# An order table in place of a list planner, and doubled values loaded by 128-partition transfers, in an attention and feed-forward kernel

## The chip, the core and the metric

The kernel runs on one core of one Trainium2 chip. TensorE (PE) multiplies matrices, VectorE (DVE), ScalarE (ACT) and GpSimd (POOL) do elementwise work, and SyncE (SP) issues most of the transfers; ScalarE issues some too. Each of these engines works through its own queue in the order in which the program was written, and waits on semaphores where a step needs another engine's result. Sixteen DMA engines move the data. The time is the device time of one execution in microseconds (us); lower is better.

## The reference

Eight sequences of 576 tokens with eight heads of width 64 go through masked attention, and the 4608 x 512 result through a feed-forward layer:

```python
scores = scale * np.matmul(q, k.transpose(0, 1, 3, 2))
mask_local = (rel >= 0) & (rel < stride)                      # heads 0-3, stride 32
mask_strided = (rel >= 0) & (pos[None, :] % stride == pos[:, None] % stride)   # heads 4-7
attn = softmax(np.where(masks, scores, -1e9)); x = np.matmul(attn, v)
h = x @ w_in                          # 512 -> 1024
solu = h * softmax(h)
ln = (solu - mean(solu)) / sqrt(var(solu) + 1e-6) * g_ln
return ln @ w_out                     # 1024 -> 512
```

`q`, `k`, `v` and `g_ln` are 4-byte floats; `w_in` and `w_out` are 8-byte floats.

## The kernel before, in words

**Attention.** For every sequence `b` there are five units of work (`UNITS`): two strided ones (the positions are permuted so that a head's residue classes are contiguous blocks of 18) and three local ones (three blocks of 64 queries with 96 keys each). A unit (`unit`, L492 to L586) computes scores on TensorE (`qk`, L509), takes the maximum and subtracts it on VectorE (L523, L524), exponentiates on ScalarE (L525), sums (L526), normalizes on GpSimd (L534), splits the probabilities into a high and a low half-precision part (L540, L542 or L544), has SyncE transpose them by DMA (`pt<-p`, L546), multiplies with the values (`pv`, L552 to L569) and splits the result into `xhi` and `xlo` (L584, L585).

**Values.** They too are needed as high and low parts, scaled by a power of two that is found from their sum of squares (`v_scale`, `v_split`). The strided values of a sequence are 768 KB as loaded, the local ones 640 KB (`vrl`). For sequence 0 the strided values are loaded twice over, into both halves of the partitions of `vtwo` (`load_v`, L425), so that the product with the high part and with the low part can be stacked; these two loads, `t0` and `t1`, are the first steps on ScalarE's queue. For sequence 0 the sum of squares comes from TensorE (`gram`, L367: each 128-column piece times itself, L379), over `vtwo` first and `vrl` second; the scale is known after that, and both value splits wait for it. For later sequences the second copy is made by transfers inside the chip (`vd<-vtwo`, `ve<-vl`, L486).

**Feed-forward.** 36 tiles of 128 tokens (`ff`, L589). The first matrix product (`g1`, L623, two halves of twelve matmuls) uses high and low parts of both operands; then come maximum, exponential, product, centring, a norm whose power is on GpSimd, a DMA transpose of the centred tile (`ct<-c`, L665), the second product (`g2`, L668) and the scaled store (L677). Tile 0 needs units 0, 1 and 2 of sequence 0 and all of `w_in`.

**Weights.** Each 8-byte float is decoded to 4 bytes in three steps (`decode`, L686: two on ScalarE, one on VectorE), `w_in` in four blocks of 128 rows, `w_out` in four of 256; then squared, scaled and split (`prep_w`, `prep_o`, `split_o`).

**What sets the order.** `add` records each of 1390 steps with its engine, an assumed duration, a key and what it reads and writes. `Plan.order` (L160) plays the steps through on the host: each engine takes, of the steps that are ready by the assumed times, the one with the smallest key; a small model of two shared transfer queues (`Queues`) gives the landing times. Keys stand in the lists `UK`, `PK`, `TK`, `GK`, `VK`, `LK`, `LF`, `LW`, `SK`. `emit` then writes the program in that order. Waits between engines are put in from the data that each step touches, whatever the order.

Of the kernel before, what the change touches and what calls it, by code (L numbers as in the profile page):

```python
# [43 lines left out]
LOAD = (8, 0.35, 1.2, 1.4)  # L44
# [3 lines left out]
LATE0 = 0.5  # L48
POOL_LO = 2
KX = -0.4  # L50
AFTER_O = [1, 1, 2, 2]
ACTQ = {"t0", "t1"}
# [3 lines left out]
UK = [  # L56
    -1.43, -0.93, -24.14, 0.24, -23.81, 0.24, -2.58, 11.29, 49.63, 17.93, 11.81, 0.92, 6.04, 10, 9.99, 12.38, 9.89, 12.65, 11.22, 13.19, 9.73, 11.19,
    20.74, 11.38, 12.09, 0.52, 12.71, 32.96, 19.98, 34.88, 33.33, 33.25, 32.84, 12.73, 26.99, 29.5, 22.87, 22.19, 31.76, 34.07,
]
PK = [  # L60
    -0.48, 11.9, -0.29, 0.88, 15.34, -1.75, -0.14, 1.46, 1.14, 0.3, -0.78, -1.14, -1.42, -6.92, 11.93, 13, 10.91, 13.83, 11.36, 4.85, 11.64, 12.7,
    12.02, -0.87, 11.97, 13.04, 13.11, 12.49, 12.49, 11.54, 11.3, 31.63, 35.51, 32.29, 37.06, 18.48, 32.43, -1, 23.48, 33.16,
]
TK = [
    0.05, 12.2, 31.9, -2.4, -0.23, -0.05, 0.24, -1.38, -0.25, 12.28, -1.81, 11.47, 10.98, -9.03, 10.67, 0.03, 12.6, 12.77, 13.16, 19.1, 30.58, 11.13,
    12.61, 32.31, 32.29, 12.99, 31.83, 31.97, 32.36, 31.96, 30.78, -3.83, 25.23, 32.01, 32.18, 67.85,
]
GK = [
    0.81, 12.13, 53.42, 0.52, 0.39, 0.81, -30.98, 1.04, -1.13, 20.08, 12.59, 32.04, 12.25, 8.26, 10.1, 9.89, 31.45, 12.29, 36.36, 31.27, 12, 36.6,
    10.78, 13.83, 33.09, 31.32, 36.94, 33.12, 33.09, 17.87, 32.04, 33.08, 52.82, 32.68, 33.96, 34.25,  # L70
]
VK = [
    0, 10.56, 12.41, 6.42, 11.99, 28.75, 3.12, 36.73,
]
LK = [
    0, 34.17, -12.99, 12.55, 12.62, 11.03, 25.29, 42.8,
]
LF = [
    -33.99, -14.63, -28.94, -18.35, 0.01, -0.82, 11.84, 1.74, 0.11,
]  # L80
LW = [
    7.65, 31.97, -0.38, -4.92, -24.77, 12.63, -0.92, -0.04,
]
SK = [
# [9 lines left out]
class Queues:  # L94


    def __init__(self):
        self.free = [3.0, 3.0]
        self.busy = [[], []]

    def move(self, q, t, work):
        mine, other = self.busy[q], self.busy[1 - q]
        start = now = max(t, self.free[q])
        shared = 0.0
        for a, b in [x for x in other if x[1] > start]:
            if work <= 0:
                break
            if b <= now:
                continue
            if a > now:  # L110
                alone = min(work, a - now)
                now, work = now + alone, work - alone
                if work <= 0:
                    break
            both = min(b - now, 2 * work)
            now, work, shared = now + both, work - both / 2, shared + both
        self.free[q] = now = now + max(work, 0.0)
        mine.append([start, now])
        if shared > 0:
            self.free[1 - q] += shared / 2  # L120
            other[-1][1] += shared / 2
        return start, now


class Plan:

    HOP = 0.4  # L130
    LATE = 3.0
    DEEP = 100
    SKIP = {"act": 0.1, "dve": 0.08, "pe": 0.07, "pool": -0.1}
# [5 lines left out]
    def add(self, eng, dur, fn, key, r=(), w=(), lock=None, dma=None, after=()):  # L139

        n = len(self.steps)
        deps = set(after)
        for x in r:
            if x in self.writer:
                deps.add(self.writer[x])
        for x in w:
            if x in self.writer:
                deps.add(self.writer[x])
# [6 lines left out]
        lock = eng == "pool" if lock is None else lock  # L155
        self.spaces.append({x[0] for x in (*r, *w) if isinstance(x, tuple) and x[0] in BANKED} if eng in ("pe", "act", "dve") else set())
        self.steps.append((eng, dur, fn, key, deps, lock, dma))
        return n

    def order(self):  # L160
        steps = self.steps
        left = [len(s[4]) for s in steps]
        users = [[] for _ in steps]
        for n, s in enumerate(steps):
            for d in s[4]:
                users[d].append(n)
        ready_at = [0.0] * len(steps)
        free = dict.fromkeys(("pe", "act", "dve", "pool", "sp"), 0.85)
        locked = dict.fromkeys(("dve", "pool"), 0.0)
        queues, moved, pieces = Queues(), 0, []  # L170
        waiting = {e: [] for e in free}
        for n, s in enumerate(steps):
            if not left[n]:
                waiting[s[0]].append(n)
        out = []
        while len(out) < len(steps):
            best = None
            for e, ns in waiting.items():
                if not ns:
                    continue  # L180
                now = max(free[e], min(ready_at[n] for n in ns))
                n = min((n for n in ns if ready_at[n] <= now), key=lambda n: (steps[n][3], n))
                if best is None or now < best[0]:
                    best = now, e, n
            now, e, n = best
            waiting[e].remove(n)
            out.append(n)
            dur = steps[n][1]
            if e == "act" and steps[n][6]:
                _, issue, begins, lands = steps[n][6]  # L190
                end = queues.move(1, now + begins, dur)[1] + lands + (LATE0 if now < 20 else self.LATE)
                free[e] = now + issue + 0.06
            elif e == "sp":
                pushes, issue, begins, lands = steps[n][6]
                start, landed = queues.move(0, now + begins, dur)
                pieces.append((start, landed, moved, moved + pushes))
                moved += pushes
                free[e] = now + issue + 0.06
                for a, b, c, d in reversed(pieces):
                    if c < moved - self.DEEP <= d:  # L200
                        free[e] = max(free[e], a + (b - a) * (moved - self.DEEP - c) / (d - c))
                        break
                end = landed + lands + (LATE0 if steps[n][6] == LOAD and now < 20 else self.LATE)
            else:
                if steps[n][5]:
                    now = max(now, locked["pool" if e == "dve" else "dve"])
                    locked[e] = now + dur
                end = now + dur
                free[e] = end - (0.16 if dur > 2.4 else self.SKIP[e])
            for m in users[n]:  # L210
                left[m] -= 1
                ready_at[m] = max(ready_at[m], end + (0.0 if steps[m][0] == e and not (e == "act" and steps[n][6]) else self.HOP))
                if not left[m]:
                    waiting[steps[m][0]].append(m)
        self.span = max(free.values())
        return out


def emit(nc, tc, plan):
# [4 lines left out]
    for n in plan.order():  # L224
        eng = plan.steps[n][0]
        k = len(nc.cur_bb.bb.instructions)
        plan.steps[n][2]()
# [3 lines left out]
        for x in sorted(plan.spaces[n]):  # L231
            true = [d for d in sorted(plan.steps[n][4]) if x in plan.spaces[d] and plan.steps[d][0] != eng]
# [12 lines left out]
def attn_solu_kernel(ctx: ExitStack, tc: tile.TileContext, qloc, qstr, kloc, kstr, vloc, vstr, w_in, w_out, g, masks, out):  # L245
# [75 lines left out]
    sk = iter(SK).__next__  # L321

# [44 lines left out]
    def gram(dst, pieces, key, w, room, scrap):  # L367
# [4 lines left out]
        for i, (x, r) in enumerate(pieces):  # L372
# [11 lines left out]
            key(), r=[A, "unit"], w=[J, w])  # L384

    def pow2_scale(dst, parts, one, key, r, w, room, top=14, mul=1.0):

        tot, T = room  # L390
# [460 lines left out]
```

## Time and profile before

| | us |
|---|---|
| median of 3 runs (513.05 to 514.99) | 514.79 |
| the profiled execution | 512.79 |
| its span, first to last instruction | 511.1 |
| TensorE busy | 473.5 |
| VectorE busy | 358.5 |
| ScalarE busy | 295.5 |
| GpSimd busy | 157.4 |

The profile is of one execution. In a table by stage each row gives the stretch, its length, busy time of PE, PEld (weight loads, which overlap matmuls), DVE, ACT and POOL with the number of instructions, the granted TensorE clock (1.00 is full speed), the mean busy share of the 16 DMA engines and what they moved in GB/s. A row in order of time is start, duration, engine, line, operation, output <- input, and in brackets how long the engine sat idle before it and what ended that. A row of waits is who waited for whom: total us, times, longest. A row of DMA issues ends with KB each and the median us from issue to landing. L379 is line 379.

### The profile page before, as it was taken

The numbers are of one execution on the slowest core, as the hardware profiler recorded it, in microseconds if no ns is written. First come the engines' busy times: TensorE is split into PE (matmuls) and PEld (weight loads), VectorE is DVE, ScalarE is ACT, GpSimd is POOL, SyncE is SP. The second block draws the span as 40 slices with busy tenths as digits, with TensorE's granted clock in tenths as the row PEclk, the third lists the DMA queues.
The fourth block names the chain that finished last, engine by engine and source line by source line (L and its number), as shares of the span: only waits on it lengthen the run. The fifth ranks groups of instructions, "written<-read, shape, count | busy, mean of one in ns | idle before, by whom it ended". The sixth has DMA issues, their size and how long they took to land.

```text
span 511.1 us, 11878 instructions
## 1 busy us (share of the span) xinstructions
PE 473.5 (93%) x4858; PEld 247.2 (48%) x4858; DVE 358.5 (70%) x679; ACT 295.5 (58%) x414; POOL 157.4 (31%) x258
## 2 busy tenths in 40 slices
PE   0538978999999999999999999999999999999997
PEld 0435544445545555454544455555544555544443
DVE  0597989768767779667994789677975789754330
ACT  1578967684546737654765666564666447554331
POOL 3164363314313214313341235212531315311210
PEclk9855989999999999999999999999999999999999
DMA  8999999739993799979885499979985697673342
GB/s 218 402 310 271 355 211 202 152 77 242 273 199 84 157 211 280 222 212 195 236 161 109 118 227 239 245 202 223 231 158 104 164 167 158 108 122 63 65 104 78
DMA packets 168294, 96.51 MB, mean 189 GB/s; under 512 B 138032, under 2 KB 154800, under 8 KB 167728
## 3 DMA queue, kind: packets, MB, share of 16 engines
q1 hardware_dynamic: 162768, 84.74, 77.9%
q10 hardware_dynamic: 5472, 11.01, 6.9%
q8 instruction: 38, 0.62, 0.5%
q14 instruction: 16, 0.13, 0.1%
HBM read 40.03 MB, written 9.44 MB: 97 GB/s over the span
## 4 chain that ended last, share of the span: by engine, by line
PE 80%; DMA 7%; DVE 5%; ACT 4%; issue 2%; POOL 1%; ACTq 0%; POOLq 0%; DVEq 0%
PE h_ps L626 11%; PE o_ps L670 11%; PE h_ps L628 11%; PE h_ps L627 11%; PE o_ps L671 10%; PE o_ps L672 10%; PE s_ps L517 5%; PE x_ps L568 5%; DMA pt<-p 3%; DMA vtwo<-vstr 3%; PE s_ps L512 2%; DMA ct<-c 2%; POOL t L534 1%; ACT w L712 1%; PE s_ps L672 1%
## 5 line engine op out<-in xcount | busy, mean ns | idle before, releaser
L626 PE MATMUL h_ps<-w,xhi 128*128 128x512 f16 x280 | 107.1, 382 | 0.6 <-DVE eu L647 0.6
L627 PE MATMUL h_ps<-w,xhi 128*128 128x512 f16 x280 | 106.7, 381 | 0.0
L628 PE MATMUL h_ps<-w,xlo 128*128 128x512 f16 x280 | 106.6, 381 | 0.0
L670 PE MATMUL o_ps<-obuf,ct 128*128 128x512 f16 x272 | 103.4, 380 | 1.0 <-DMA ct<-c 1.0
L672 PE MATMUL o_ps<-obuf,ct 128*128 128x512 f16 x272 | 103.1, 379 | 0.0
L671 PE MATMUL o_ps<-obuf,ct 128*128 128x512 f16 x272 | 103.1, 379 | 0.0
L534 POOL TENSOR_TENSOR t<-t,m 128x576 f32<-128x576 f32 (+2 forms) x40 | 56.2, 1404 | 139.4 <-DVE m L531 111.4
L633 DVE TENSOR_REDUCE st<-h_ps 128x1 f32<-128x1024 f32 x35 | 42.8, 1222 | 42.5 <-PE h_ps L628 42.5
L652 DVE SCALAR_TENSOR_TENSOR c<-eu,st,c 128x1024 f16<-128x1024 f32 x36 | 48.8, 1354 | 25.3 <-ACT c L651 24.1
L644 ACT ACTIVATE eu<-h_ps,st,vsc 128x1024 f32<-128x1024 f32 x31 | 37.3, 1204 | 43.3 <-DVE st L634 43.3
L651 ACT ACTIVATE c<-eu,st 128x1024 f16<-128x1024 f32 x36 | 41.2, 1146 | 28.0 <-DVE st L650 26.0
L647 DVE SCALAR_TENSOR_TENSOR eu<-h_ps,st,eu 128x1024 f32<-128x1024 f32 x35 | 44.8, 1280 | 8.8 <-ACT eu L644 8.4
L660 POOL TENSOR_SCALAR st<-st 128x1 f32<-128x1 f32 x36 | 18.7, 520 | 103.2 <-ACT junk L654 102.0
L540 ACT CAST p<-t 128x576 f16<-128x576 f32 (+2 forms) x40 | 26.9, 674 | 33.2 <-POOL t L534 32.6
L628 PEld LDWEIGHTS <-xlo 128*128 128x128 f16 x288 | 28.3, 98 | 34.5 <-issue 0.8
L672 PEld LDWEIGHTS <-ct 128*128 128x128 f16 x288 | 28.2, 98 | 34.0
L626 PEld LDWEIGHTS <-xhi 128*128 128x128 f16 x288 | 28.2, 98 | 33.7 <-DVE eu L647 0.7
L670 PEld LDWEIGHTS <-ct 128*128 128x128 f16 x288 | 28.1, 98 | 33.1 <-DMA ct<-c 1.1
L627 PEld LDWEIGHTS <-xhi 128*128 128x128 f16 x288 | 28.3, 98 | 31.3 <-issue 0.6
L517 PE MATMUL s_ps<-k,q 64*54 64x54 f32 (+1 forms) x1280 | 41.4, 271 | 2.2 <-DMA q<-qloc 2.2
L671 PEld LDWEIGHTS <-ct 128*128 128x128 f16 x288 | 28.2, 98 | 30.2
L654 ACT ACTIVATE junk<-eu,st 128x1024 bf16<-128x1024 f32 x36 | 40.9, 1137 | 0.8 <-ACT ob L678 0.8
(148 smaller groups left out, 707.6 us busy)
## 6 DMA issues: line engine op xcount, KB each, us to landing
out<-ob ACTq DMA_DIRECT2D x36, 256.0 KB, 3.9
vtwo<-vstr SPq DMA_DIRECT2D x7, 768.0 KB, 6.6
vd<-vtwo SPq DMA_DIRECT2D x14, 384.0 KB, 8.8
vrl<-vloc SPq DMA_DIRECT2D x8, 640.0 KB, 5.6
q<-qstr SPq DMA_DIRECT2D x8, 594.0 KB, 5.4
k<-kstr SPq DMA_DIRECT2D x8, 594.0 KB, 6.8
k<-kloc SPq DMA_DIRECT2D x8, 576.0 KB, 6.0
q<-qloc SPq DMA_DIRECT2D x8, 576.0 KB, 4.2
```

The lines of the kernel that those rows point to most:

```text
L517: nc.tensor.matmul(s_ps[row : row + nq, pair, i * nk : (i + 1) * nk], q_raw[half][hs, q0 : q0 + (nq - 1) * nqb + 1 : nqb], k_raw[half][hs, ...
L534: add("pool", nx * nk / 510 + 0.02, lambda: nc.gpsimd.tensor_tensor(tv, tv, sm.unsqueeze(2).broadcast_to([P, nx, nk]), op=ALU.mult), key + ...
L626: nc.tensor.matmul(hv[:, i], xhi[:, cc, tok], whi[:, cc, cols], start=(cc == 0), stop=False)
L627: nc.tensor.matmul(hv[:, i], xhi[:, cc, tok], wlo[:, cc, cols], start=False, stop=False)
L628: nc.tensor.matmul(hv[:, i], xlo[:, cc, tok], whi[:, cc, cols], start=False, stop=(cc == 3))
L633: add("dve", 1.21, lambda: nc.vector.tensor_reduce(low, hv, axis=AX.XY, op=ALU.max, negate=True), key + 0.2, r=HH, w=[(ST, "low")])
L647: add("dve", 1.3, lambda: nc.vector.scalar_tensor_tensor(uv, hv, ia, ev, op0=ALU.mult, op1=ALU.mult, accum_out=us), key + 0.3, r=[*HH, E, ...
L651: add("act", 1.2, lambda: nc.scalar.activation(c[:, 0], u, AF.Identity, bias=mean, scale=1.0), key + 0.35, r=[U, (ST, "mean")], w=[(C, 0)])
L652: add("dve", 1.28, lambda: nc.vector.scalar_tensor_tensor(c[:, 1], u, mean, c[:, 0], op0=ALU.add, op1=ALU.subtract), key + 0.4, r=[U, (ST, ...
L670: nc.tensor.matmul(o, ct[:, cc, :], ohi[:, cc, :], start=(cc == 0), stop=False)
L671: nc.tensor.matmul(o, ct[:, cc, :], olo[:, cc, :], start=False, stop=False)
L672: nc.tensor.matmul(o, ct[:, 8 + cc, :], ohi[:, cc, :], start=False, stop=(cc == 7))
```

## The change

1. `Queues`, the playing-through in `Plan.order`, all keys and all assumed durations go. A table `ORDER` of 1390 step numbers takes their place, and `order` returns it after an assertion that each step stands behind what it depends on. The steps themselves, their engines and their instructions are the same; a condition that held the loads of `w_out` behind two transposes in the planner (`after`, `AFTER_O`) goes with it.
2. The two loads of `vtwo` are cut the other way. Before, `t0` filled partitions 0 to 63 and `t1` partitions 64 to 127, each with both column halves. After, `t0` fills the first column half and `t1` the second, each in all 128 partitions, from a source that is read twice. What is said to read and write which half follows that.

```diff
-UK = [
+ORDER = [
+    13, 1, 0, 31, 14, 10, 11, 7, 9, 5, 15, 19, 6, 2, 4, 3, 32, 33, 58, 12, 8, 34, 17, 16, 69, 18, 23, 27, 59, 70, 71, 60, 72, 61, 82, 62, 63, 20, 73, 95, 74,
...
     def order(self):
-        steps = self.steps
-        left = [len(s[4]) for s in steps]
...
+        place = {n: i for i, n in enumerate(ORDER)}
+        assert sorted(ORDER) == list(range(len(self.steps)))
+        assert all(place[d] < place[n] for n, s in enumerate(self.steps) for d in s[2])
+        return ORDER
...
-    def load(name, dst, src, us, key, w, after=()):
+    def load(name, dst, src, w):
         e, q = ("act", nc.scalar) if name in ACTQ else ("sp", nc.sync)
-        add(e, us, lambda: q.dma_start(dst, src), key, w=w, dma=LOAD, after=after)
+        add(e, lambda: q.dma_start(dst, src), w=w)
...
-    def load_v(b, a, key, key2=None):
+    def load_v(b, a):
         if b == 0 and a:
-            for i in range(2):
-                load(f"t{i}", vtwo[i * D : i * D + D].rearrange("p (y f) -> p y f", y=2), vstr[b].rearrange("(y p) f -> p y f", y=2), 1.95,
-                     key2 if i else key, [("vr2", 1)] if i else [("vr", 1), ("v", 1, 0), ("v", 1, 1)])
+            for y in range(2):
+                f = slice(y * 6 * 4 * D, (y + 1) * 6 * 4 * D)
+                src = vstr[b][y * D : y * D + D].unsqueeze(0).broadcast_to([2, D, 6 * 4 * D])
+                load(f"t{y}", vtwo[:, f], src, [("vr2", 1), ("v", 1, 0), ("v", 1, 1)] if y else [("vr", 1)])
             return
...
     def v_split(b, a, key):
         if b == 0 and a:
             raw = vtwo.rearrange("p (y c f) -> p c y f", y=2, c=6)
-            R = [("vr", 1), ("vr2", 1), ("vsc", 0), ("v", 1, 0), ("v", 1, 1)]
             for y in range(2):
-                hi, lo = vd_sb[:, 0, :, y], vd_sb[0:D, 1, :, y]
+                hi, lo, R = vd_sb[:, 0, :, y], vd_sb[0:D, 1, :, y], [("vsc", 0), *([("vr2", 1), ("v", 1, 0), ("v", 1, 1)] if y else [("vr", 1)])]
```

Worked out from the keys and from the table, the first steps on the queues that the prediction speaks of (w0 to w3: the blocks of `w_in`; wo: of `w_out`; q1, k1 strided, q0, k0 local; a sequence's number in brackets; u0 to u4 the units of sequence 0):

| queue | before | after |
|---|---|---|
| SyncE | q1, mask, k1, w3, local v, w2, g, k0, w0, q0, w1; then q1(1), k1(1), three `ve` copies, transpose u0, local v(1), strided v(1), transposes u1 and u2, wo, wo, transpose u3, wo, wo | w3, k1, mask, q1, local v, w0, k0, q0, g, w1, w2; then local v(1), transpose u0, a small `ve` copy, strided v(1), wo, k1(1), wo, q1(1), transpose u1, a `ve` copy, wo, transpose u2, the large `ve` copy, wo |
| TensorE | squares of `vtwo`, scores u0, squares of local v, scores u1, scale, ... products u2, scores of unit 6, products u3, first feed-forward tile | squares of `vtwo`, scores u0, squares of local v, scale, scores u1, u2 and u3, ... products u2, scores of unit 6, first feed-forward tile, products u3 |
| ScalarE | t0, t1, decode w3 (two), exponential u0, decode w2 (two), strided split, local split, ... | t0, t1, decode w3 (two), exponential u0, half of the decode of w0, local split, strided split, ... |
| VectorE | scores u0 (two steps), last step of w3, ... | last step of w3, scores u0 (two steps), ... |

Over the whole run the steps that leave the longest common order of the two versions are 61 of 250 on TensorE, 136 of 329 on ScalarE, 224 of 531 on VectorE, 31 of 95 on GpSimd and 81 of 185 on SyncE. On TensorE and SyncE the last eight steps are the same but for one swap on TensorE; the last scaling and store stay last.

More of the change, by code (lines that the diff above doesn't have):

```diff
@@ L64 @@
[L64 to L84, printed above, removed]
[4 rows of a table removed]
+ORDER = [
[48 rows of a table added]
 ]
 BANKED = ("h", "x")
[L94 to L122, printed above, removed]
@@ L137, in __init__, with add @@
         self.writer, self.readers = {}, {}
-    def add(self, eng, dur, fn, key, r=(), w=(), lock=None, dma=None, after=()):
+    def add(self, eng, fn, r=(), w=()):
         n = len(self.steps)
-        deps = set(after)
-        for x in r:
+        deps = set()
+        for x in (*r, *w):
             if x in self.writer:
@@ L167, in order @@
[L167 to L214, printed above, removed]
@@ L226, in emit @@
         k = len(nc.cur_bb.bb.instructions)
-        plan.steps[n][2]()
+        plan.steps[n][1]()
         if not plan.spaces[n]:
@@ L231, in emit @@
         for x in sorted(plan.spaces[n]):
-            true = [d for d in sorted(plan.steps[n][4]) if x in plan.spaces[d] and plan.steps[d][0] != eng]
+            true = [d for d in sorted(plan.steps[n][2]) if x in plan.spaces[d] and plan.steps[d][0] != eng]
             for i in new:
@@ L338, in masks_bf16, with load_masks @@
         nc.vector.tensor_copy(mk_str, m[:, 2:3, 0:QS].broadcast_to([P, 6, QS]))
-    def load_masks(key):
-        load("mask", mask_sb, masks, 0.4, key, ["mask_raw"])
-        add("dve", 1.0, masks_bf16, key, r=["mask_raw"], w=["mask"])
-    add("pool", 1.6, lambda: nc.gpsimd.memset(vd_sb[D:P, 1].bitcast(F32), 0.0), -9, w=["vz"])
+    def load_masks():
+        load("mask", mask_sb, masks, ["mask_raw"])
+        add("dve", masks_bf16, r=["mask_raw"], w=["mask"])
+    add("pool", lambda: nc.gpsimd.memset(vd_sb[D:P, 1].bitcast(F32), 0.0), w=["vz"])
     for i in range(NPB):
@@ L400, in pow2_scale @@
             one = parts.bitcast(BF16)[:, 1:2]
-        add("pe", 0.15, lambda: nc.tensor.matmul(tot, ones, one, start=True, stop=True), key(), r=["ones", *r], w=[T])
+        add("pe", lambda: nc.tensor.matmul(tot, ones, one, start=True, stop=True), r=["ones", *r], w=[T])
         def root():
@@ L674, in ff @@
         for i in range(2):
-            add("pe", 2.75, lambda i=i: g2(i), key2, r=[CT, *(("o_w", cc) for cc in range(4 * i, 4 * i + 4))], w=[O])
+            add("pe", lambda i=i: g2(i), r=[CT, *(("o_w", cc) for cc in range(4 * i, 4 * i + 4))], w=[O])
         def store():
@@ L679, in store, with decode @@
             nc.scalar.dma_start(out[n * P : (n + 1) * P, :], ob)
-        add("act", 1.06, store, key2 + 0.3, r=[O, (ST, "f")], w=[OB])
+        add("act", store, r=[O, (ST, "f")], w=[OB])
     ROOMS = [(eu_sb[i].bitcast(I32), [("e", i), ("u", i)]) for i in range(2)] + [(rooms[i], [("room", i)]) for i in range(2)]
-    def decode(dst, src, w, room, n, after=()):
+    def decode(dst, src, w, room, n):
         room, RAW = room
@@ L728, in prep_o @@
     def prep_o():
-        add("pool", 0.3, lambda: nc.gpsimd.tensor_tensor(gg_sb[:, 0], g_sb, g_sb, op=ALU.mult), sk(), r=["g"], w=["gg"])
+        add("pool", lambda: nc.gpsimd.tensor_tensor(gg_sb[:, 0], g_sb, g_sb, op=ALU.mult), r=["g"], w=["gg"])
         for i in range(4):
             dst, D2 = o32[:, 2 * i : 2 * i + 2], [("od", 2 * i), ("od", 2 * i + 1)]
-            decode(dst, w_out[2 * i * P : (2 * i + 2) * P].rearrange("(c p) (f t) -> p c f t", c=2, t=2), D2, ROOMS[(i + 2) % 4], 4 + i,
-                   [turned[AFTER_O[i]]] if AFTER_O[i] is not None else [])
@@ L734, in prep_o @@
-        k = sk()
-        add("dve", 0.17, lambda: nc.vector.tensor_reduce(gm[:, 0:1], gg_sb[:, 0], axis=AX.X, op=ALU.max), k, r=["gg"], w=["gm0"])
-        add("pe", 0.2, lambda: nc.tensor.matmul(o_ps[0:1, 0:P], gm.bitcast(BF16)[:, 1:2], unit_sb, start=True, stop=True), k, r=["gm0", "unit"], w=["o"])
-        add("dve", 0.2, lambda: nc.vector.tensor_reduce(gm[0:1, 1:2], o_ps[0:1, 0:P], axis=AX.X, op=ALU.max), k, r=["o"], w=["gm1"])
-        add("pe", 0.2, lambda: nc.tensor.matmul(o_ps[:, 0:1], ones[0:1], gm.bitcast(BF16)[0:1, 3:4], start=True, stop=True), k, r=["ones", "gm1"], w=["o"])
@@ L744, in prep_o @@
-        pow2_scale(o_sc, o_sc[:, 4:5], None, lambda: k, ["om"], "o_sc", (o_ps[:, 0:1], "o"))
-        add("dve", 0.15, lambda: nc.vector.tensor_scalar(gg_sb[:, 1], g_sb, o_sc[:, 1:2], None, op0=ALU.mult), k, r=["g", "o_sc"], w=["go"])
+            decode(dst, w_out[2 * i * P : (2 * i + 2) * P].rearrange("(c p) (f t) -> p c f t", c=2, t=2), D2, ROOMS[(i + 2) % 4], 4 + i)
+        add("dve", lambda: nc.vector.tensor_reduce(gm[:, 0:1], gg_sb[:, 0], axis=AX.X, op=ALU.max), r=["gg"], w=["gm0"])
+        add("pe", lambda: nc.tensor.matmul(o_ps[0:1, 0:P], gm.bitcast(BF16)[:, 1:2], unit_sb, start=True, stop=True), r=["gm0", "unit"], w=["o"])
@@ new lines, in prep_o @@
+        add("dve", lambda: nc.vector.tensor_reduce(gm[0:1, 1:2], o_ps[0:1, 0:P], axis=AX.X, op=ALU.max), r=["o"], w=["gm1"])
+        add("pe", lambda: nc.tensor.matmul(o_ps[:, 0:1], ones[0:1], gm.bitcast(BF16)[0:1, 3:4], start=True, stop=True), r=["ones", "gm1"], w=["o"])
+        add("dve", lambda: nc.vector.tensor_copy(gm[:, 2:3], o_ps[:, 0:1]), r=["o"], w=["gm"])
+        pieces = [(o32[:, 2 * i : 2 * i + 2].rearrange("p c f -> p (c f)"), [("od", 2 * i), ("od", 2 * i + 1)]) for i in range(4)]
```

245 lines of the change are left out of this document (104 added, 141 removed), and 51 rows, old and new, of tables (ORDER, SK).

## The prediction

> **What bounds the kernel now.** I read the head of the page first, then busy time by stage, then what TensorE waited for, then the first 60 us in order of time.
>
> ```profile
> span 511.1 us, 11878 instructions
> ...
> PE 473.5 (93%) x4858; PEld 247.2 (48%) x4858; DVE 358.5 (70%) x679; ACT 295.5 (58%) x414; POOL 157.4 (31%) x258
> ```
>
> The stages are cut where TensorE starts (14.55), where the first feed-forward matmul starts (57.01), where its last early wait ends (81.75) and where it finishes (507.43). Columns: length, busy time of each engine, granted clock, DMA share, GB/s.
>
> ```profile
> 0.00:14.55 14.55, 0.00 (x1) 0.03 (x1) 1.18 (x6) 1.28 (x1) 4.44 (x26) 1.00 0.90 230
> 14.55:57.01 42.46, 28.77 (x519) 22.05 (x520) 34.24 (x66) 34.12 (x40) 16.20 (x12) 0.68 1.06 324
> 57.01:81.75 24.74, 20.53 (x238) 11.49 (x235) 22.26 (x45) 19.25 (x27) 13.84 (x14) 0.93 1.16 264
> 81.75:507.43 425.68, 424.16 (x4107) 213.65 (x4106) 300.81 (x563) 240.15 (x346) 122.92 (x207) 1.00 0.82 171
> 507.43:511.07 3.64, 0.00 (x0) 0.00 (x0) 0.00 (x0) 0.69 (x1) 0.00 (x0) 0.94 0.19 72
> ```
>
> From 81.75 on TensorE is busy 424.16 of 425.68 us at full clock. An order can win 1.5 us there. The 3.6 us after TensorE's end are the last scaling and store, whose steps keep their place. All else lies before 81.75: 32.4 us in which TensorE does nothing (14.55 + 13.69 + 4.21), and a clock of 0.68 in the second stage. Its waits:
>
> ```profile
> PE o_ps L379 <- DMA vtwo<-vstr: 14.5, 1, 14.5
> PE x_ps L568 <- DMA pt<-p: 4.6, 3, 2.2
> ...
> PE s_ps L517 <- DMA q<-qloc: 2.2, 1, 2.2
> ```
>
> Nearly half of the 32.4 is one wait: the first step on TensorE's queue squares the doubled values (`vtwo`), and they land at 14.5. What hangs behind it, in order of time:
>
> ```profile
> 14.55 2.72 PE L379 MATMUL o_ps<-vtwo 128*128 128x128 bf16 x24 [14.55 <-DMA vtwo<-vstr]
> ...
> 17.47 1.42 PE L517 MATMUL s_ps<-k,q 64*54 64x54 f32 x48
> ...
> 17.17 1.19 ACT L695 ACTIVATE ct<-room 128x1024 f32<-128x1024 f32 x1 [13.68 <-DMA room<-w_in]
> ...
> 20.70 0.75 ACT L525 ACTIVATE t<-t 128x648 f32<-128x648 f32 x1 [1.22 <-DVE t L524]
> ...
> 57.01 0.39 PE L626 MATMUL h_ps<-w,xhi 128*128 128x512 f16 x1
> ```
>
> From the first exponential (20.70) to the first feed-forward matmul ScalarE hardly rests, and its gaps are waits for VectorE and GpSimd:
>
> ```profile
> 20.70:57.01 36.31, 23.62 (x433) 17.31 (x433) 32.55 (x64) 31.81 (x38) 16.20 (x12) 0.62 1.07 309
> ```
>
> So the head is a load of 14.5 us, 6.15 us to the first exponential, then 36.3 us set by ScalarE (31.81 busy) and VectorE (32.55).
>
> **The change, part by part.** *The planner and its keys* run on the host. Removing them costs nothing on the chip. No step is added or dropped and no instruction gets another shape, except the two loads of `vtwo`. What changes is the order on each queue and those loads.
>
> *The two loads* move 2 x 768 KB as before, in rows of 6144 bytes, on ScalarE's DMA queue. Before, each fills 64 partitions, and the outermost dimension of both patterns is 64. After, each fills 128 partitions, and the source begins with a dimension of 2: the two copies, stride zero. Here is how fast memory comes in while the old loads run, and after:
>
> ```profile
> 0.00:2.00 2.00, 0.00 (x0) 0.00 (x0) 0.20 (x2) 0.00 (x0) 1.26 (x14) 1.00 0.19 33
> ...
> 8.00:10.00 2.00, 0.00 (x0) 0.00 (x0) 0.00 (x0) 0.00 (x0) 0.00 (x0) 1.00 1.00 231
> ...
> 12.00:14.00 2.00, 0.00 (x0) 0.00 (x0) 0.00 (x0) 0.00 (x0) 0.00 (x0) 1.00 1.02 261
> 14.00:16.00 2.00, 1.45 (x15) 1.48 (x16) 0.00 (x0) 0.00 (x0) 0.00 (x0) 1.00 1.02 423
> 16.00:18.00 2.00, 2.00 (x40) 1.76 (x41) 0.00 (x0) 0.83 (x1) 0.00 (x0) 1.00 1.02 417
> ```
>
> The engines are full (share 1.0) all along, but move 231 to 261 GB/s until `vtwo` has landed and 417 to 423 after it. So half-partition loads cost the whole chip nearly half its rate. What is loaded then:
>
> ```profile
> room<-w_in SPq DMA_DIRECT2D x2, 1024.0 KB, 16.2
> eu<-w_in SPq DMA_DIRECT2D x2, 1024.0 KB, 13.7
> vtwo<-vstr ACTq DMA_DIRECT2D x2, 768.0 KB, 10.6
> vrl<-vloc SPq DMA_DIRECT2D x1, 640.0 KB, 15.6
> q<-qstr SPq DMA_DIRECT2D x1, 594.0 KB, 4.4
> k<-kstr SPq DMA_DIRECT2D x1, 594.0 KB, 13.0
> k<-kloc SPq DMA_DIRECT2D x1, 576.0 KB, 13.1
> q<-qloc SPq DMA_DIRECT2D x1, 576.0 KB, 13.0
> mask<-masks SPq DMA_DIRECT2D x1, 144.0 KB, 9.5
> ```
>
> `vtwo` is 1.57 MB; SyncE's eleven first loads (with `g`) are 7.40 MB, and none waits for compute. The price of the new loads hangs on how many of the 16 DMA engines each is dealt out to, and no row shows a transfer that begins with a dimension under 16. I bound it from both sides.
>
> *All sixteen:* 417 GB/s from 1.9 us on (the first 2 us carry 33 GB/s). The two queues got about equal shares before (230 GB/s x 14.55 us = 3.35 MB, of which `vtwo` 1.57), so `vtwo` lands after 3.15 MB, at 9.4 us: 5.1 earlier.
>
> *Two, one for each copy:* an engine moves 417/16 = 26.1 GB/s. The two loads put 0.786 MB on each of the two, 30.2 us, and SyncE's loads a sixteenth each, 0.462 MB, 17.7 us. `vtwo` lands at 1.9 + 30.2 = 32.1 if it never shares, at 49.8 if all of SyncE's loads pass first. By the equal shares above, 0.462 passes before 0.786 is through: I take 49.8.
>
> I take the second bound. The transfer has to be cut into shares along some dimension that both patterns have; the old 64 gives sixteen shares of four, the new 2 gives two. That is a judgement, not a reading. The Trainium skill (DMA: Bandwidth & Descriptors, "Why a DMA increments its semaphore by 16 and not by 1") says that the engine count is the largest number up to 16 that divides the slowest dimension of both patterns, which would be 2 here; no run yet shows it. By that rule the sum is the one below, without it the first rival's.
>
> *The order.* In front of the first feed-forward matmul ScalarE does the same steps as before from the first exponential on, plus one exponential (0.68): 31.81 + 0.68 = 32.5 us. VectorE gets some 2.4 us more. On TensorE's queue squaring `vtwo` is still first and the scores of unit 0 follow it, so neither can cover a late `vtwo`. ScalarE decodes one block of `w_in` (two instructions) and then stands at that unit's exponential; VectorE stands behind the same scores. SyncE's twelfth step reloads `vrl`, which must first be split with a scale that needs `vtwo`; all later loads and transposes queue behind it. So the whole head slides with `vtwo`:
>
> - squaring at 49.8 instead of 14.55;
> - first exponential 6.15 later, at 56.0;
> - first feed-forward matmul after 32.5 us of ScalarE, at 88.5 with no gap, 93.0 with the old gaps (36.31 - 31.81 = 4.5). I take no gap: `w_in` is long there, and no decode waits for a load.
>
> That is 88.5 - 57.0 = +31.5 us. Later, unit 3's product falls behind the first feed-forward tile instead of before it, about 0.7 on TensorE (a local unit's product, below); a wait or two of the third stage may go. I set both to nothing against each other.
>
> ```profile
> 93.07 0.69 PE x_ps L568 x36
> ...
> PE o_ps L670 <- DMA ct<-c: 1.0, 1, 1.0
> PE s_ps L401 <- DVE vs L394: 0.3, 1, 0.3
> ```
>
> The last two rows are all that TensorE waits for from 81.75 to 507.4. Over the whole run some 60 of TensorE's 250 steps change their place among the others, most by one, and some 80 of SyncE's 185. A gain here is at most 1.5; a loss has no such bound, but a swapped product has half a tile of queued matmuls on either side to hide in. I take 0, ends -1.5 and +4.
>
> Sum: 511.1 + 31.5 = 542.6 span. The profiled execution took 512.79, 1.7 over its span, and the median of the runs (514.79) lies 2.0 above that: 542.6 + 3.7 = 546. Its own range: 528 (32.1 landing, 511.1 + 13.7 + 3.7) to 552 (with the gaps and half a microsecond to a few of the later stage).
>
> **The rivals.**
>
> *Sixteen engines, and the order fits (not slower).* `vtwo` lands at 9.4. Unit 0's scores need 2.42 MB of SyncE's queue (the first `w_in` block is now ahead of k, mask and q) and 1.57 beside: 3.99 MB, at 11.5, inside the squaring that ends at 12.1. First exponential at 9.4 + 6.15 = 15.6, feed-forward at 48.1 to 52.6: 4.4 to 8.9 us won, less 0.7. I take 6: 505 span, 509; own range 504 to 512. For it: the doubling from 261 to 423 GB/s the moment that `vtwo` is in. Against it: the leading 2. It decides from ten engines on: 0.157 MB of `vtwo` on each and as much of SyncE's beside are 12.1 us, a landing at 14.0.
>
> *The loads gain nothing.* The 231 to 261 comes from two queues sharing, not from the partitions. Then the 3.99 MB take 16.6 us at 240, unit 0's scores start at 18.5 instead of 17.5, and the better order after that gives about the same back: 512 to 517. Against it: at 16 us SyncE's loads alone ran at 417.
>
> *Sixteen engines, but a new wait in SyncE's queue.* The largest of the three shifted copies of the local values stood ahead of all loads of `w_out`; it is now behind three of them (3.1 MB) and unit 2's transpose, and unit 2's product, which gates the first feed-forward matmul, needs it. About 14.7 MB lie ahead of it: 37 us at 417, 47 at the second stage's 324, 58 at the third's 264. Only the last is later than 57.0; with the rest it makes 2 to 5 us: 518. For it: 264 GB/s is what the DMA did once transposes were dense. Against it: before 57 they are few.
>
> **How the numbers follow.** Two engines 0.58, sixteen and a fitting order 0.27, no gain 0.07, new wait 0.08. A measurement of this kernel tells about 0.5% (2.6 us) from no change. Faster 0.27 (the second case), same 0.08 (the third and a little of the last), slower 0.65. The predicted time is the first case's. As both signs hold weight, the range spans 504 to 552: outside are the best of the second case and the worst of the first, about a tenth. The first case's own range is 528 to 552.
>
> **What would show it.** The wait of TensorE for `vtwo` reads near 50 us in the first case (32 at least), near 9.5 in the second, near 14.5 in the third. In the first the DMA share falls to about an eighth once SyncE's loads are through, before TensorE has started, and `vtwo`'s issue-to-landing time is over 30 us. The stretch from squaring to the first feed-forward matmul should stay 38 to 43 us in either of the first two. From then on TensorE should idle under 6 us; more of it, behind transposes or `ve`, is the fourth case. A `vtwo` that lands before 20 makes the prediction wrong; so does a head in which TensorE finds other work before it.

## The result, and the profile after

The changed kernel takes 542.84 us (median, 542.55 to 543.32) against 514.89 (513.05 to 515.87, with a fourth run) for the kernel before: a ratio of 1.0548, with a 95% interval of 1.0518 to 1.0579. Its profiled execution has a span of 540.8 us, 29.7 more than the 511.1 before. The head of the page after:

```profile
span 540.8 us, 11844 instructions
...
PE 472.9 (87%) x4858; PEld 247.4 (46%) x4858; DVE 356.7 (66%) x679; ACT 293.8 (54%) x414; POOL 147.6 (27%) x258
```

TensorE does as much as before (472.9 us against 473.5), so all of the loss is time in which it stands still. Busy time by stage shows where. The stages are cut where TensorE first has half of `vtwo` (30.97), where it has the other half (50.42), at the first feed-forward matmul (90.77), at 115 and at TensorE's end. Columns as before: length, PE, PEld, DVE, ACT, POOL, granted clock, DMA share, GB/s.

```profile
0.00:30.97 30.97, 0.00 (x1) 0.01 (x1) 2.28 (x7) 3.48 (x3) 4.37 (x26) 1.00 0.47 160
30.97:50.42 19.45, 1.46 (x13) 1.19 (x13) 0.00 (x0) 0.00 (x0) 0.00 (x0) 1.00 0.33 98
50.42:90.77 40.35, 26.90 (x472) 20.13 (x472) 33.01 (x63) 32.23 (x38) 14.64 (x11) 0.94 0.91 271
90.77:115.00 24.23, 22.99 (x281) 12.68 (x281) 23.40 (x44) 19.40 (x29) 9.80 (x11) 0.95 1.24 245
115.00:537.20 422.20, 421.50 (x4096) 213.38 (x4094) 298.00 (x567) 238.01 (x346) 118.77 (x210) 1.00 0.81 172
```

For 50 us next to nothing is computed: TensorE is busy 1.5 us of it, VectorE 2.3 and ScalarE 3.5. The first feed-forward matmul comes 33.8 us later than before (90.77 against 57.01), and from there to the end the kernel needs 450.0 us in place of 454.1, 4.0 less. What TensorE waited for, in us in total, times, longest:

```profile
PE o_ps L295 <- DMA vtwo<-vstr: 49.0, 2, 31.0
PE x_ps L472 <- issue: 4.8, 1, 4.8
PE s_ps L418 <- DVE t L430: 3.7, 2, 2.0
```

It waits twice for `vtwo`, since the squaring of the first column half no longer needs the second load. In order of time on TensorE, and for ScalarE's first exponential:

```profile
30.97 1.46 PE L295 MATMUL o_ps<-vtwo 128*128 128x128 bf16 x12 [30.97 <-DMA vtwo<-vstr]
50.42 1.46 PE L295 MATMUL o_ps<-vtwo 128*128 128x128 bf16 x12 [17.99 <-DMA vtwo<-vstr]
...
55.31 0.74 ACT L431 ACTIVATE t<-t 128x648 f32<-128x648 f32 x1 [47.28 <-DVE t L430]
...
88.18 0.37 PE L472 MATMUL x_ps<-pt,ve 96*64 96x64 f16 x6 [4.77 <-issue]
...
90.77 0.61 PE L530 MATMUL h_ps<-w,xhi 128*128 128x512 f16 x1
```

And the transfers while TensorE stands, the last three columns being clock, DMA share and GB/s:

```profile
20.00:30.00 10.00, 0.00 (x0) 0.00 (x0) 0.00 (x0) 0.00 (x0) 0.00 (x0) 1.00 0.13 53
...
40.00:50.00 10.00, 0.00 (x0) 0.00 (x0) 0.00 (x0) 0.00 (x0) 0.00 (x0) 1.00 0.12 49
```

A share of 0.13 is that of two engines out of sixteen, and 53 GB/s is then 26.5 for each of them. Read so, fourteen engines are idle while two carry `vtwo` and their own part of SyncE's loads; the share is a mean, and the packets counted further down bear the reading out.

SyncE stands too. Its queue in order of time (start, duration of the issue):

```profile
3.43 0.49 SPq L237 DMA_DIRECT2D eu<-w_in  x1
30.94 0.33 SPq L237 DMA_DIRECT2D k<-kloc  x1
31.31 0.43 SPq L237 DMA_DIRECT2D q<-qloc  x1
50.39 0.33 SPq L237 DMA_DIRECT2D g<-g  x1
```

After six loads it issues nothing for 27 us, and its waits name `vtwo` as the cause:

```profile
SPq L237 <- DMA vtwo<-vstr: 45.6, 2, 27.0
```

### The profile page after: what moved, and what is told of

It reads as the page before. It is cut to its first block, busy times and chain, and to the rows that moved or that the text cites. A ratio compares the mean times of both kernels' runs of the same rounds, so it can differ in the third digit from the quotient of the medians.

```text
span 540.8 us, 11844 instructions
## 1 busy us (share of the span) xinstructions
PE 472.9 (87%) x4858; PEld 247.4 (46%) x4858; DVE 356.7 (66%) x679; ACT 293.8 (54%) x414; POOL 147.6 (27%) x258
## 4 chain that ended last, share of the span: by engine, by line
PE 75%; DMA 11%; DVE 9%; ACT 2%; issue 1%; ACTq 0%; DVEq 0%
PE o_ps L573 11%; PE o_ps L574 10%; PE o_ps L575 10%; PE h_ps L530 10%; PE h_ps L532 10%; PE h_ps L531 10%; DMA vtwo<-vstr 9%; PE s_ps L423 5%; PE x_ps L472 4%; DMA pt<-p 1%; PE s_ps L418 1%; DVE obuf L652 1%; DMA ct<-c 1%; DVE obuf L600 1%; DVE m L432 1%
## 5 line engine op out<-in xcount | busy, mean ns | idle before, releaser
L440 POOL TENSOR_TENSOR t<-t,m 128x576 f32<-128x576 f32 (+2 forms) x40 | 49.3, 1233 | 269.3 <-DVE m L437 208.3
L431 ACT ACTIVATE t<-t 128x576 f32<-128x576 f32 (+2 forms) x40 | 27.3, 685 | 73.6 <-DVE t L430 73.3
L429 DVE TENSOR_REDUCE m<-s_ps 128x6 f32<-128x576 f32 (+2 forms) x40 | 30.1, 752 | 46.3 <-PE s_ps L423 46.2
L556 DVE SCALAR_TENSOR_TENSOR c<-eu,st,c 128x1024 f16<-128x1024 f32 x36 | 47.4, 1316 | 9.4 <-ACT c L555 9.3
L295 PE MATMUL o_ps<-vtwo 128*128 128x128 bf16 x24 | 2.9, 306 | 49.0 <-DMA vtwo<-vstr 49.0
L575 PEld LDWEIGHTS <-ct 128*128 128x128 f16 x288 | 28.2, 98 | 34.0
L573 PEld LDWEIGHTS <-ct 128*128 128x128 f16 x288 | 28.1, 98 | 32.7 <-DMA ct<-c 0.6
```

What stands on the lines that cost most here:

```text
L440: add("pool", lambda: nc.gpsimd.tensor_tensor(tv, tv, sm.unsqueeze(2).broadcast_to([P, nx, nk]), op=ALU.mult), r=TM, w=[T])
L556: add("dve", lambda: nc.vector.scalar_tensor_tensor(c[:, 1], u, mean, c[:, 0], op0=ALU.add, op1=ALU.subtract), r=[U, (ST, "mean"), (C, 0)] ...
L573: nc.tensor.matmul(o, ct[:, cc, :], ohi[:, cc, :], start=(cc == 0), stop=False)
L575: nc.tensor.matmul(o, ct[:, 8 + cc, :], ohi[:, cc, :], start=False, stop=(cc == 7))
```

## The experiments

**Which half of the change: the loads or the table?** Two theories were set against each other. The *loads*: the leading dimension of 2 puts each `vtwo` load on two engines, and the table costs nothing. The *order*: the table's queues lose the time. Four kernels separate them: each order with the old loads, with the new ones, and with a third form. In that form the doubled values stand as 128 rows in an input of their own, so that each load is a plain one of 128 partitions; the doubling is then part of how the input is laid out, and not of the timed execution.

The table with the old loads:

```diff
-                f = slice(y * 6 * 4 * D, (y + 1) * 6 * 4 * D)
-                src = vstr[b][y * D : y * D + D].unsqueeze(0).broadcast_to([2, D, 6 * 4 * D])
-                load(f"t{y}", vtwo[:, f], src, ...
+                src = vstr[b].rearrange("(y p) f -> p y f", y=2)
+                load(f"t{y}", vtwo[y * D : y * D + D].rearrange("p (y f) -> p y f", y=2), src, ...
```

> The table of 1390 steps as changed, but the two `vtwo` loads put back to the old form (each fills 64 partitions with both value bands). Theory of the loads (the new pattern runs on two of sixteen engines, and the table costs nothing): `vtwo` lands at about 14.5 us as before, the first feed-forward matmul comes at about 57, and the span is 505 to 511 us, a ratio of 0.985 to 1.00. Rival, the order: the table itself makes the kernel slower (its SyncE queue puts the large `ve` copy behind the `w_out` loads, and a product waits 4.8 us); then the span stays at 530 us or more with `vtwo` landing at about 14.5. If the order is worth what the changed kernel's part after the first feed-forward matmul shows (450.0 us against 454.1), the span is 507.

The planner with the new loads (the same lines the other way, in the kernel before):

> The kernel before, list planner and keys and all, with only the two `vtwo` loads put in the new form (band doubled over 128 partitions, source pattern beginning with the dimension of 2). Theory of the loads: TensorE waits for `vtwo` until about 50 us, the first feed-forward matmul comes at about 90, the DMA share falls to about 0.13 once the other loads are through, and the time is 541 to 550 us (ratio 1.05 to 1.07). Rival, the order: about 515 us, ratio 1.00, since the queue and the keys are those of before.

The table with plain loads from a doubled input:

```diff
-                src = vstr[b][y * D : y * D + D].unsqueeze(0).broadcast_to([2, D, 6 * 4 * D])
-                load(f"t{y}", vtwo[:, f], src, ...
+                load(f"t{y}", vtwo[:, f], vtwice[:, f], ...
```

> The changed kernel with the doubled values laid out as 128 rows in an input of their own, so that each `vtwo` load is a plain load of 128 partitions whose outermost dimension is 128; the same bytes are moved into the chip. Theory of the two engines: all sixteen engines are used, `vtwo` lands at about 9.5 to 10.5 us, the first feed-forward matmul comes at 48 to 53, and the span is 501 to 507 us (ratio 0.975 to 0.99). Rival, the rate is set by the two queues sharing the memory and not by the pattern: `vtwo` lands at about 14.5 as in the kernel before and the span is 507 to 511. Rival, the order: 530 or more.

The planner with the same plain loads:

> The kernel before with the planner's order and the doubled values as plain loads of 128 partitions from an input of their own. It measures what faster `vtwo` loads are worth without the table. If the first feed-forward matmul moves with the landing of `vtwo` (about 4 to 5 us earlier), the time is 509 to 512 us, ratio 0.99 to 0.995; if other waits of the first stage (`pt`, `q`, the transposes in TensorE's order) take the gain, 513 to 515, ratio 1.00. The difference to the same loads under the table is what the table is worth.

Medians, with the ratio to the kernel before and its interval. The four were measured on one chip, where the kernel before took 513.79 us; the changed kernel's own row is that of the result above, so ratios are compared.

| `vtwo` loads | planner | table |
|---|---|---|
| old, 64 partitions | 1 | 510.95, 0.9946 (0.992 to 0.9971) |
| new, source begins with 2 | 552.45, 1.0755 (1.0706 to 1.0804) | 542.84, 1.0548 (1.0518 to 1.0579) |
| plain, 128 rows from a doubled input | 509.75, 0.9909 (0.9876 to 0.9942) | 505.3, 0.9822 (0.9796 to 0.9848) |

The theory of the loads holds and the theory of the order falls. The new loads make either order slower by 6 to 8%; the table makes every row faster, by 0.5, 1.9 and 0.9%. In the middle row more than half of the 8.0 us between the two profiles lie ahead of the first feed-forward matmul, which comes at 95.15 under the planner and at 90.77 under the table; there the second half of `vtwo` lands at 54.2 and 50.4. The first waits of TensorE, of the table with old loads, the planner with new loads, and the table with plain loads:

```profile
PE o_ps L295 <- DMA vtwo<-vstr: 16.5, 1, 16.5
```

```profile
PE o_ps L379 <- DMA vtwo<-vstr: 52.8, 2, 30.6
```

```profile
PE o_ps L295 <- DMA vtwo<-vtwice: 10.3, 2, 8.3
```

A part of the expectations was off. With the old loads under the table `vtwo` is there at 16.5 and not at 14.5, and the planner with the new loads is 2.5 us slower than the 541 to 550 given. The same bytes through the same queue in plain form are waited for a fifth as long, so the form of the load alone makes the wait.

**Where the table wins.** From the first feed-forward matmul to the end the planner takes 453.7 to 454.1 us (three kernels) and the table 450.0 to 450.5 (three kernels), whatever the loads. The waits of TensorE in that stretch, of the kernel before and then of the changed one:

```profile
PE x_ps L568 <- DMA pt<-p: 3.6, 2, 2.2
PE o_ps L670 <- DMA ct<-c: 1.0, 1, 1.0
PE h_ps L626 <- DVE eu L647: 0.6, 1, 0.6
PE s_ps L401 <- DVE vs L394: 0.3, 1, 0.3
```

```profile
PE x_ps L472 <- DVE xlo L489: 1.2, 1, 1.2
PE h_ps L530 <- DVE eu L551: 0.4, 1, 0.4
```

5.5 us of waits have become 1.6. The difference of 3.9 is what the stretch lost in length (4.0). The two products that waited for transposed probabilities (`pt`) no longer do.

**Is it the leading dimension, or that rows are read twice?** The new load has both: it begins with 2, and that dimension has stride zero. Here it begins with 4, over 32 rows, and with 16, over 8 rows. Bytes, queue and place are the same, but sequence 0 is then computed from repeated rows. These two and the next kernel have one run each:

```diff
-                src = vstr[b][y * D : y * D + D].unsqueeze(0).broadcast_to([2, D, 6 * 4 * D])
+                src = vstr[b][y * D : y * D + 32].unsqueeze(0).broadcast_to([4, 32, 6 * 4 * D])
```

> The changed kernel with one number of the load's source altered: the broadcast dimension that leads it is 4 (four times the same 32 rows) in place of 2 (twice the same 64 rows), so that sequence 0 is computed from repeated rows; bytes, queue, place and everything else are the same. Theory that the leading dimension sets the number of DMA engines: four of sixteen engines, a plateau of about 105 GB/s and a DMA share of about 0.25 where `vtwo` moves alone, twice the 53 GB/s of the changed kernel; the two loads together need about 15 us alone on their engines, `vtwo` lands at 25 to 30 us, and the time is 518 to 524 us. Rival, that reading a row twice at once (the zero stride) is what is slow: about 53 GB/s again and 541 to 545 us.

> As the case before, with a leading broadcast dimension of 16 (sixteen times the same 8 rows). Theory of the leading dimension: all sixteen engines, about 410 GB/s through the first stage, `vtwo` lands at about 10 to 12 us and the time is 504 to 509 us, as with the host-doubled plain loads (505.3). Rival of the zero stride: 541 to 545 us.

And the other way round: no row read twice, but two blocks that can't be merged, from the doubled input with a spare row behind every 64:

```diff
-                load(f"t{y}", vtwo[:, f], vtwice[:, f], ...
+                load(f"t{y}", vtwo[:, f], vtwice.rearrange("(h p) f -> h p f", h=2)[:, 0:D, f], ...
```

> The host-doubled input again, right values, no row read twice, but laid out with one spare row after every 64 so that the load's source is two blocks of 64 rows that can't be taken as one dimension of 128. Theory of the leading dimension: two engines, `vtwo` waited for until about 50 us and 540 to 546 us, as in the changed kernel. Rival of the zero stride: sixteen engines and 504 to 508 us, as with the plain load (505.3).

The two blocks take 542.51 us, with the changed kernel's span (540.8) and its wait to the tenth:

```profile
PE o_ps L295 <- DMA vtwo<-vtwice: 49.0, 2, 31.0
...
20.00:30.00 10.00, 0.00 (x0) 0.00 (x0) 0.00 (x0) 0.00 (x0) 0.00 (x0) 1.00 0.13 53
```

With a leading 4 it is 531.19 us. The transfers by stretch, while other loads share (8 to 16) and while `vtwo` is nearly alone:

```profile
8.00:12.00 4.00, 0.00 (x0) 0.00 (x0) 0.00 (x0) 0.52 (x1) 0.00 (x0) 1.00 1.02 236
12.00:16.00 4.00, 0.00 (x0) 0.00 (x0) 0.00 (x0) 0.00 (x0) 0.00 (x0) 1.00 1.07 220
18.00:22.00 4.00, 0.00 (x0) 0.00 (x0) 2.12 (x6) 0.00 (x0) 0.00 (x0) 1.00 0.27 102
32.00:38.00 6.00, 0.00 (x0) 0.00 (x0) 0.00 (x0) 0.00 (x0) 0.00 (x0) 1.00 0.25 100
```

With a leading 16 it is 508.18 us, and `vtwo` is complete at 15.2:

```profile
8.00:12.00 4.00, 0.80 (x8) 0.80 (x9) 0.00 (x0) 0.33 (x1) 0.00 (x0) 1.00 1.04 252
12.00:16.00 4.00, 1.43 (x15) 1.17 (x13) 0.62 (x3) 0.00 (x0) 0.00 (x0) 1.00 1.01 280
16.00:20.00 4.00, 3.14 (x69) 2.59 (x68) 3.04 (x6) 0.00 (x0) 0.00 (x0) 1.00 1.02 421
```

Two, four and sixteen give shares of 0.13, 0.25 and 1.0 and 53, 100 and 250 to 300 GB/s. For sixteen the share alone proves little, since SyncE's loads run at the same time and fill it. The packets on ScalarE's DMA queue over the whole run tell more; of the changed kernel, with 4 and with 16 (packets, MB, share):

```profile
q10 hardware_dynamic: 5444, 11.01, 6.2%
q10 hardware_dynamic: 5448, 11.01, 6.8%
q10 hardware_dynamic: 5472, 11.01, 7.1%
```

The bytes are the same to the hundredth of a MB, the old loads have 5472 too, and the two blocks without repeated rows 5444. In the trace the two loads are 256 packets of 6144 bytes and, beside these, 4, 8 and 32 packets of 4 bytes: two, four and sixteen for each load. That one such packet stands for one engine is my reading; the shares of 0.13 and 0.25 fit it.

So the leading dimension sets the number of engines, with a stride of zero or without. The Trainium skill's rule (DMA: Bandwidth & Descriptors, "Why a DMA increments its semaphore by 16 and not by 1"), that the engine count is the largest number up to 16 that divides the slowest dimension of both patterns, agrees with all three. My expectation for 4 was 7 us short (518 to 524): it counted the bytes at 26 GB/s on each engine, and while the loads are mixed the engines move less, as the first two of its rows show. For 16 the time was as expected (504 to 509), but not the way: I had given 410 GB/s and a landing at 10 to 12.

**Is the old loads' low rate that of half the partitions?** With 16 engines the changed pattern still runs at 252 to 302 GB/s beside SyncE's loads, where the plain form, complete at 11.7, ran at this:

```profile
8.00:12.00 4.00, 1.72 (x15) 1.46 (x16) 0.10 (x1) 2.24 (x2) 0.00 (x0) 1.00 1.02 414
12.00:16.00 4.00, 4.00 (x74) 3.44 (x72) 2.93 (x8) 0.00 (x0) 0.00 (x0) 1.00 1.04 428
```

So two queues at once are not what slows: in the first row both are at work. Two more kernels, with old halves in plain form (one run), and with the old loads on two queues at the same time:

```diff
-                load(f"t{y}", vtwo[:, f], vtwice[:, f], ...
+                load(f"t{y}", vtwo[y * D : y * D + D], vtwice[y * D : y * D + D], ...
```

> The table with the host-doubled input, but each `vtwo` load now fills 64 partitions with 12 KB rows (the lower half of the partitions first, then the upper) where the plain loads fill 128 with 6 KB rows. Bytes, queue and input are the same, values right. If filling half of the partitions is what held the memory to 231 to 261 GB/s in the kernel before, the rate beside these loads is about 240 GB/s again, TensorE waits for `vtwo` until 14 to 17 us and the time is 509 to 512 us. If it was the source (each row of `vstr` read twice by the old loads, 48 KB read sixteen times by the one with a leading 16), the rate is about 410 GB/s, `vtwo` is there at about 10 and the time is 505.

```diff
-ACTQ = {'t0', 't1'}
+ACTQ = {'t0'}
 ORDER = [
-    13, 1, 0, 31, 14, 10, ...
+    13, 14, 1, 0, 31, 10, ...
```

> The table with the old half-partition loads from `vstr` (510.95 us, ratio 0.9946), but the second half is issued on SyncE's queue, first of its loads, so that both halves are filled at the same time from two queues; no doubled input. If half of the partitions is the limit, the two halves together run at about 400 GB/s, `vtwo` is there at 6 to 8 us, the other loads follow at full rate, and the time is 502 to 506 us (ratio 0.975 to 0.985). If the reading is the limit, about 240 GB/s, `vtwo` at 8.5 to 9 and the scores' loads a little later: 505 to 509. If two queues at once are the limit whatever they load, no better than 510.

Halves from the doubled input take 510.6 us. The rate is that of the old loads until they have landed, and then full:

```profile
8.00:12.00 4.00, 0.00 (x0) 0.00 (x0) 0.00 (x0) 1.54 (x2) 0.00 (x0) 1.00 1.00 212
12.00:16.00 4.00, 0.00 (x0) 0.00 (x0) 0.00 (x0) 0.00 (x0) 0.00 (x0) 1.00 0.98 244
16.00:20.00 4.00, 3.69 (x60) 3.47 (x64) 2.12 (x6) 0.00 (x0) 0.00 (x0) 1.00 1.03 419
```

No row is read twice there, and input, bytes and queue are those of the plain loads at 414 GB/s. The rows are 12 KB in place of 6, but the old loads had 6 KB rows and were as slow. So it is the 64 partitions. Both halves at once take 508.67 us, 0.988 (0.9831 to 0.9928), with `vtwo` at 11.6, and don't run at 400:

```profile
2.00:8.00 6.00, 0.00 (x0) 0.00 (x0) 0.00 (x0) 0.83 (x1) 3.05 (x8) 1.00 0.96 209
8.00:12.00 4.00, 0.37 (x4) 0.40 (x5) 0.00 (x0) 0.00 (x0) 0.00 (x0) 1.00 1.01 244
12.00:16.00 4.00, 2.35 (x23) 2.20 (x21) 0.27 (x2) 2.17 (x2) 0.00 (x0) 1.00 1.00 398
```

That both halves together cover all partitions doesn't help. I had expected 400 GB/s and 502 to 506 us here if the half partitions are the limit, and 240 GB/s if the reading is; the second is what came, though the kernel with halves in plain form had just ruled the reading out for one load at a time. Either each half-partition load is slow for itself, or two loads that read the same rows at once are; no run separates the two. It still wins over the kernel before: of the 2.1 MB that are in by 11.6 us (6 us at 209 GB/s, 3.6 at 244), 1.57 are `vtwo`. The Trainium skill (SBUF — State Buffer, "Can I just issue two DMAs to hit both halves?") says no to just this, and that only one transfer that spans all 128 partitions reaches every port of the memory; the 209 to 244 GB/s here agree. But 64 partitions are not the only way to a low rate at a full share: a leading 4 and a leading 16, which fill all 128, have it too (220 to 236 and 252 to 302 GB/s). Why was not tried further: either the place of each engine's rows in the partitions or that several engines read the same rows could be it.

**The stall before unit 2's product.** In the table kernels TensorE stands 2.6 to 4.8 us just ahead of the first feed-forward matmul, at the product that needs the large copy of the local values (`ve`). In the kernel before that copy is issued at 29.5, ahead of all `w_out` loads; under the table it comes at 42.1, behind three of them. Two edits of the table with plain loads move it. The first moves both later copies up to the first:

```diff
-    ..., 21, 99, 24, ...   ..., 45, 168, 98, 106, ...   ..., 50, 97, 269, ...
+    ..., 21, 99, 97, 98, 24, ...   ..., 45, 168, 106, ...   ..., 50, 269, ...
```

> The table with the host-doubled plain loads (505.3 us, ratio 0.9822), and in the table two steps moved: the second and the large `ve` copy stand right behind the first one, ahead of the `w_out` loads, as in the planner's order. There unit 2's product waited 4.8 us, until 50.7, for something that the profile shows only as issue; the large copy was issued at 42.1 and took about 8.5 us to land. If that copy is what it waited for, the stall shrinks to what the transposed probabilities (issued at 39.9) set, 0 to 3 us are left, and the kernel gains 2 to 4 us: 501 to 503.5 us. If another transfer ends there, or the two copies now delay the loads behind them, no gain: 505 to 506.

The second moves the large one alone, behind the other (`168, 98, 97, 106`), and was run beside the unmoved kernel on one chip:

> The table with host-doubled plain loads once more, beside the next kernel on one chip, as the two were 505.3 and 506.5 on different chips: 504 to 506.5 us, ratio 0.982, an interval that overlaps that of the first time.

> As that, with one step of the table moved and no more: the large `ve` copy stands right behind the second small one, ahead of one `w_out` load and unit 2's transpose. It is issued at about 37.6 in place of 42.1. If the copy's late landing is what the 4.8 us stall before unit 2's product costs, TensorE waits there only for the transposed probabilities (0 to 3 us) and the kernel gains 2 to 4 us against the same kernel without the move: ratio 0.975 to 0.979. If, as when two copies were moved, the stall goes but the granted clock falls in its place, no gain: ratio 0.981 to 0.985.

Unit 2's product in the unmoved kernel, with both copies moved, and with the large one moved:

```profile
50.74 0.38 PE L471 MATMUL x_ps<-pt,ve 96*64 96x64 f16 x6 [4.78 <-issue]
```

```profile
51.14 0.28 PE L424 MATMUL x_ps<-pt,ve 96*64 96x64 f16 x6 [0.24 <-DMA pt<-p]
```

```profile
50.03 0.37 PE L424 MATMUL x_ps<-pt,ve 96*64 96x64 f16 x6 [2.56 <-DMA pt<-p]
```

The copy was the cause: moved, it is waited for no more, and what ends last there is `pt`. But the time stays: 506.48 us, 0.9832 (0.9801 to 0.9863) with both moved, 505.55, 0.9813 (0.9777 to 0.9849) with one, against 505.73, 0.982 (0.9781 to 0.986) unmoved. My expected gain of 2 to 4 us is not there. With one moved, the product starts 0.7 us earlier (0.8 against a second profile of the unmoved kernel, which has it at 50.80 after 3.3 us of idle time), as `pt` lands hardly before the copy did. With both moved, a load behind them comes late. SyncE issues the next sequence's `vtwo` at 28.06 in place of 26.65, ScalarE's sum of squares over it waits 2.1 us for it, and TensorE waits behind that, where the unmoved kernel's profiles have 0.2 at most:

```profile
PE s_ps L268 <- DVE vs L261: 2.0, 1, 2.0
```

From there on the transposes go 1.8 us later (unit 2's at 41.77 in place of 39.92), and the product starts at 51.14. TensorE's granted clock reads lower as well, 0.60 in place of 0.91 from 36 us to the first feed-forward matmul, and it is busy 14.6 us there in place of 9.5, in part because more work falls behind 36 us (211 matmuls in place of 186). That the clock cost time is not shown: the last thing waited for is `pt`, and of this kernel's six runs the one with the highest mean clock (0.988) took longest, 509.09.

## Why the prediction was right

The forecast was 546 us (own range 528 to 552), and 542.84 was measured. Step by step:

- *Two engines for each `vtwo` load.* Right, and shown: share 0.13, 53 GB/s, and the runs with 2, 4 and 16. What was given as a judgement is now measured.
- *`vtwo` lands at 49.8.* Measured 50.4, but the way there was partly luck. I let all eleven of SyncE's first loads pass on the two engines (17.7 us). Only eight did, 5.3 MB or 12.7 us, since SyncE itself was held at 30.94 and 50.39 by landings of `vtwo`. That gives 1.9 + 30.2 + 12.7 = 44.8. The other 5.6 us are a lower rate than 26.1 GB/s for each engine. While SyncE's loads keep all engines busy, these move only 15 to 17 GB/s each:

```profile
10.00:12.00 2.00, 0.00 (x0) 0.00 (x0) 0.00 (x0) 0.00 (x0) 0.00 (x0) 1.00 1.08 273
12.00:14.00 2.00, 0.00 (x0) 0.00 (x0) 0.00 (x0) 0.00 (x0) 0.00 (x0) 1.00 0.95 251
...
32.00:34.00 2.00, 0.43 (x4) 0.16 (x2) 0.00 (x0) 0.00 (x0) 0.00 (x0) 1.00 0.95 266
34.00:36.00 2.00, 0.00 (x0) 0.00 (x0) 0.00 (x0) 0.00 (x0) 0.00 (x0) 1.00 1.01 241
```

If the two engines were slowed there as the sixteen were on average, these 8 us cost 3.1 against 417 GB/s, which is an estimate. The rest is not placed.

- *6.15 us from the squaring to the first exponential.* 4.9 (50.42 to 55.31): half of the squaring was done at 31.
- *Then 32.5 us of ScalarE with no gap.* ScalarE was busy 32.23 us, so the count of its steps was right, but the stretch took 35.5 (55.31 to 90.77). For 2.9 us of the gap ScalarE stood waiting for unit 2's product, which TensorE's stall of 4.8 us held back. That was the mechanism of my fourth case, the shifted copy behind the `w_out` loads; it came true inside the first case, as a part of it. I had excluded gaps because "`w_in` is long there". That was not so: two of its four blocks were issued only at 50.76 and 51.24. They were in before ScalarE came to them, and no decode waited, but I had looked at that transfer alone.
- *Head +31.5 us.* Measured +33.8: 0.6 from the landing, -1.3 from the squaring, +3.0 from the gap.
- *Later stages 0 (ends -1.5 and +4).* Mis-sized: it measured -4.0. I gave 1.5 us to what an order can win after 81.75, and set "a wait or two of the third stage" to nothing against the 0.7 of unit 3's product. Those waits, two for `pt`, were 3.6 us, and the table took both.
- *The sum.* 542.6 was the span forecast and 540.8 the span: +2.3 for the head and -4.0 behind it. I added 2.0 for the way from the profiled execution to the median; the profiled execution (542.55) and the median lie 0.3 us apart this time.

The second case (sixteen engines and a fitting order, 504 to 512) is what the plain loads measured: 505.3. Its landing of 9.4 was 2.3 early: the second half is there at 11.7. The third case (the loads gain nothing) fell: plain loads ran at 414 GB/s beside the other queue, so two queues are not what made 231 to 261.

## What to carry to other kernels

Look at the outermost dimension of both sides of a transfer before its bytes: a broadcast that stands outermost with a size of 2 leaves fourteen of sixteen engines idle, and a DMA share of an eighth in the profile is its mark. A transfer that covers more partitions isn't better for that if it is dealt out to fewer engines; here the doubled rows in memory, loaded as 128 plain rows, gave what the change had meant to give, with the table 1.8% under the kernel before, though something outside the timed execution must then lay them out. When a wait is taken away, ask which landing is next in line (behind the `ve` copy it was `pt`, 0.7 us ahead of it), and what the moved transfer now stands in front of.

## What had not been expected of the hardware

- In this program a queue can be held by a transfer of another engine's queue. With eight transfers issued (two by ScalarE, six by SyncE) SyncE's next one waits for the first `vtwo` to land, at 30.94, though its own first load had landed by 5.8 (ScalarE decodes that block at 5.83). The plain loads and the leading 16 and 4 show the same: the ninth goes at 8.28, 11.17 and 23.86, where TensorE's first wait for `vtwo` ends. In the kernel before it goes at 9.23. So a slow load at the head stops later loads that share no byte with it. Releasers are inferred from semaphores; whether the chip asks for this wait, or only the way in which this program uses its semaphores, no run tells.
- Loads that fill 64 partitions hold all that runs beside them to 209 to 261 GB/s with the engines' share between 0.96 and 1.02, also when both halves run at once.
- The granted clock in the first 60 us differs between kernels that do nearly the same work there (0.60 against 0.91 above), and even between two profiles of one kernel (the table with plain loads: 1.00 and 0.83 from 40 to 50 us). No run here tells what sets it, and none shows that it cost time.
